# A fused attention and token-MLP kernel: the condition's load and one pair of token tiles on ScalarE's queue, idle matmuls in four pieces in front of the first columns, and a new order of all steps

## The chip, the core and the metric

The kernel runs on one core of one Trainium2 chip. The metric is the device time of one execution in microseconds (us). The core has five engines with an instruction stream each: TensorE (PE in the profile, its weight loads PEld), VectorE (DVE), ScalarE (ACT), GpSimd (POOL) and SyncE (SP). Each runs its own stream in order and waits on semaphores for the others. DMAs are issued here from SyncE's queue (SPq) and, for a few loads and stores, from ScalarE's (ACTq).

## What is computed

One adaLN block over a sequence of S = 2048 tokens of D = 512 channels in bfloat16: a sliding, dilated local attention (part A), and behind it an MLP that mixes tokens (part B).

```
mod = silu(c) @ w_mod                      # c: 1 x 512; six vectors of 512
sa, ca, ga, sb, cb, gb = mod
h = layernorm(x) * (1 + ca) + sa
q, k, v = h @ wqkv                         # 32 heads of 16
logits[s, w] = q[s] . k[s - 2w] / 4        # w = 0..7, masked where s - 2w < 0
x = x + ga * (softmax(logits) over the 8 keys, times v) @ wo
h = layernorm(x) * (1 + cb) + sb
u = gelu(layernorm(h)^T @ w1 + b1)         # over tokens: 2048 -> 1792
x = x + gb * (u @ w2 + b2)^T               # 1792 -> 2048
```

## The kernel before

The 2048 tokens are 16 tiles of 128. Part A goes through them in five chunks of 2, 4, 4, 4 and 2 tiles (`SIZES`); part B needs all tokens for each output and is split in three groups of columns of hidden units, accumulated in PSUM, with partial sums parked in SBUF.

At the start the condition `c` is loaded (`ld_c`, into the tile `c_t`), turned into a column by a small matmul (`cps`), and put through silu by an exponential on ScalarE (`silu_exp`) and three steps on VectorE (`silu_dve`). Two sets of 16 one-column matmuls (`modcols1`, `modcols0`; the tile `psS<-sc,big`) make the scale `a1col` and the shift `sab`; the third part of the modulation is made later as rows (`modrow0`, `modrow1`). `act_table` is an explicit load of ScalarE's function table (ACT_TABLE_LOAD).

For each chunk: statistics of each tile (`ln1s`, `ln1v`: BATCH_NORM_STATS2 and BATCH_NORM_AGGREGATE on VectorE, or two accumulating activations into `junk` on ScalarE), `rstd`, `nb`, normalized tiles (`n1`, into `h`), transposes by TensorE (`tr`, `psS<-ident,h`), evictions of them (`hT`), twelve projections or fewer (`qkv`), their evictions (`ev`, into `q_sb`, `k_f`, `v_sb`; `qvb` is the bias that stems from the shift). Then, on VectorE, four products of query and shifted keys of all eight windows (`qk`, the tile `big<-q_sb,k_f`: 128 x 4096 elements in chunks of four tiles, 128 x 2048 in chunks of two), summed over a head's channels by TensorE (`red`, `psL<-big,group`), the softmax (`max`, `sub`, `exp`, `esum`, `rcp`, `smB`), copies of the weights (`a2`, DMA) and of the values (`vd`, DMA) in the layout of the second product, four products with values (`pv`, `big<-a2sb,vD`) and their sums by TensorE (`pvacc`), the output projection (`wo`, `psS<-woq,o_sb`) with the residual added through the identity, and the layer norms of part B (`x1`, `ln2`, `n2`, `aff`, `ln3`, `h3`). Part B is `mlp1` (with `park`, `inj`, `padd`, `gelu`), then `mlp2`, `fin` and `st_out`.

All steps are written down as entries of a graph by `add` and `add_any`; an entry of `add_any` has alternatives on several engines. `dma2` adds a load that may be issued from SyncE's or ScalarE's queue. The order is not planned at run time: `schedule` (line 86) walks the string `ORDER` (lines 191 to 248) and issues the steps in that order; each engine's stream is the order of its own tokens. A letter behind a token picks the engine (`a`, `d`, `p`, `s` for ScalarE, VectorE, GpSimd, SyncE); for a step of TensorE, `q` does it as four matmuls of 32 columns each, which run at the same time in the four column groups, and `n` leaves out a matmul for the residual, which VectorE then adds. PSUM slots (six), the four `big` and five `vD` slots are given out in the order of the tokens.

The token `fill:N` puts idle matmuls on TensorE, N pieces of 128 columns of the identity by itself, in matmuls of four pieces and a remainder of single ones (`fill_fn`, line 528):

```
for r in [4] * (n // 4) + [1] * (n % 4):
    nc.tensor.matmul(psS[k][:, 0:r * P], lhsT=ident[:], rhs=ident[:]..., start=True, stop=True)
```

All instructions are recorded at line 142, where a helper passes them on, so in the profile the tiles' names tell the steps apart.

Of the kernel before, what the change touches and what calls it, by code (L numbers as in the profile page):

```python
# [13 lines left out]
P = 128  # L14
S, D, H, DH, NW, DIL, F = 2048, 512, 32, 16, 8, 2, 1792
# [27 lines left out]
class _Graph:  # L43
# [7 lines left out]
    def add(self, eng, dur, fn, **kw):  # L51
        return self.add_any([(eng, dur, fn)], **kw)
# [149 lines left out]
ev1_02:a biascols n1_6:p ld_wrow1 rcp0 smB0 ev1_12:a ld_x_4_14 ln1s14:a qkv1_22 qk1_2 a2_0_2:a xt6 ld_wrow3 modrow1
red1_1 a2_0_1:a n1_9:p wsc2_0:d ln1s15:a ln1v14 nb1_3 n1_11:a qkv1_23:q mrows1 qkv1_21 ev1_21:a red1_2 red1_3 xt8
ev1_23:a fill:1 n1_10:p qkv1_20 ev1_20:a ev1_22:a qkv2_13 qkv2_10 wsc0_1:p vd0_2 ev2_13:a ln1v15 vd0_1 max1 sub1
qkv2_00 exp1 a2_0_0:s a2_0_3:s pv0_1 vd0_0 pv0_0 st_row0 pv0_2 qkv2_03 esum1:q ld_wo3 pvacc0_0 vd0_3 halo_v2:p
biascols_cp:a pvacc0_1 pv0_3 pvacc0_2 pvacc0_3 ev2_10:a ev2_00:a qk2_0 n1_13:a n1_12:a ld_row0 woq_s rcp1 smB1
oev0_2:a qkv2_11 qkv2_02:q ev2_03:a qk2_3 qkv2_01:q red2_0 oev0_0:a wo0:q wsc2_1:a wsc2_2:a qkv2_12 ev2_11:a ev2_01:a
ev2_02:a ev2_12:a wo1 qkv2_21:q a2_1_1:a qkv2_22 x1_1:a ln2q1:a x1_0:a xt10 ln2q0:a qk2_1 qkv2_23 xt12 qk2_2 a2_1_0:s
halo_k3:a ln2m0 vd1_2 a2_1_2:s qkv3_12 a2_1_3:s pv1_2 rstd1_4 red2_1 nb1_4 vd1_0 st_row1 red2_2 red2_3 rstd2_0
ev2_22:a nb2_0 ev2_21:a qkv3_13:q ev3_13:a max2 vd1_3 pv1_0 n1_14:a vd1_1 pvacc1_2 n1_15:a qkv2_20:q ev2_20:a sub2  # L210
qkv3_22:q ev3_12:a pv1_1 qkv3_10 exp2 ev2_23:a halo_v3:a qkv3_20 n2_0:a oev1_2:a ev3_10:a esum2 rcp2 qkv3_00 ev3_22:a
qkv3_02:q ev3_00:a pv1_3 ev3_02:a pvacc1_0 ev3_20:a qkv3_01:q ev3_01:a qkv3_11:q xt14 ld_row1 n2_1:p vd2_3 pvacc1_1
smB2 aff0 qk3_0 vd2_1 fill:1 vd2_0 oev1_0:a oev1_1:a pvacc1_3 ev3_11:a qk3_1 qkv3_23:q oev1_3:a a2_2_2:s ln3s1:a
qkv3_03:q wo4 a2_2_1:s qk3_2 a2_2_0:s ev3_03:a ev3_23:a x1_4:a ln2q4:a wo2 x1_2:a a2_2_3:s red3_0 wo3:q x1_3:a ln2q3:a
qkv3_21:q ev3_21:a wo5 red3_1 pv2_3 x1_5:a vd2_2 qk3_3 qkv4_20:q red3_2 qkv4_22 red3_3 qkv4_12 fill:18 ln2q5:a
ld_w1_0_512 ln2q2:a ln2m2 pv2_0 pvacc2_0 vd3_0 ev4_20:a ln3s0:a ln3v0 ev4_12:a rstd2_2 ev4_22:a ln3v1 qkv4_02 oev2_0:a
ln2m4 rstd2_4 nb2_2 n2_2:a max3 sub3:q exp3 pvacc2_3 oev2_3:a qkv4_10:q pv2_2 vd3_2 esum3 nb2_4 pv2_1 vd3_1 n2_3:p
ld_w1_0_0 n2_5:a rcp3 smB3 pvacc2_2 fill:14 a2_3_0:s a2_3_1:s a2_3_3:s n2_4:a qkv4_00:q oev2_2:a rstd3_0 aff2 pvacc2_1
oev2_1:a wo6 wo9 wo7 aff4 nb3_0 ln3s2:d ev4_02:a ln3s3:a ln3v3 h3_1:p wo8 a2_3_2:s ev4_00:a ln3v2 ld_w2_0 ln3s4:d
rstd3_2 nb3_2 x1_9:a ln3s5:a h3_0:p mlp1_0_6_0:q x1_7:a ln3v4 x1_8:a h3_3:d mlp1_0_1_0 h3_2:d mlp1_0_6_2 mlp1_0_1_2  # L220
pv3_1 mlp1_0_5_0:q ln3v5 ev4_10:a ld_w1_0_896 x1_6:a mlp1_0_3_0:q mlp1_0_3_2:q ln2q7:a pvacc3_1 rstd3_4 mlp1_0_5_2:q
oev3_1:a mlp1_0_2_0:q pv3_0 mlp1_0_2_2:q nb3_4 h3_4:a mlp1_0_0_0:q mlp1_0_0_2 h3_5:a mlp1_0_0_4:q qk4_0 ln2q8:a
ln2q6:a park0_0:a ln2q9:a mlp1_0_6_4:q mlp1_0_2_4:q mlp1_0_1_4:q park0_1:a pv3_2 mlp1_0_5_4:q vd3_3 pvacc3_0 oev3_0:a
mlp1_0_3_4:q ld_w2_1 park0_2:a pv3_3 red4_0 ln2m6 pvacc3_2 oev3_2:a mlp1_0_4_0:q qk4_1 pvacc3_3 ld_w1_0_1152
mlp1_0_4_2:q mlp1_0_4_4:q rstd2_6 oev3_3:a wo12:q halo_v4:p vd4_2 vd4_3 nb2_6 n2_9:a qk4_2 n2_7:d qk4_3 wo10:qn red4_1
ld_w1_0_1408 n2_6:a vd4_1 n2_8:a aff6 red4_2 red4_3 max4 park0_3:a ln3s8:d ln3s6:d x1_12:a ln3v8 wo11 vd4_0 ln3s9:d
mlp1_0_7_0 ld_w2_3 park0_4:a ln3v6 mlp1_0_7_2 park0_5:a ln3v9 x1_11:a ln2q12:a mlp1_0_8_0 mlp1_0_8_2 park0_6:a wo13:n
ln3s7:a ln3v7 sub4 mlp1_0_10_0 mlp1_0_9_0 x1_13:d exp4 rstd3_6 nb3_6 esum4 mlp1_0_8_4 ln2q13:a ln2m12 mlp1_0_10_2
mlp1_0_10_4 mlp1_0_9_2 rcp4 mlp1_0_7_4 h3_8:d rstd2_12 mlp1_0_12_0 mlp1_0_12_2 mlp1_0_12_4 smB4 a2_4_1:a a2_4_0:s
mlp1_0_9_4 a2_4_2:s h3_9:d a2_4_3:a h3_7:d nb2_12 h3_6:p mlp1_0_7_6 ln2q11:a park0_7:a x1_10:d mlp1_0_8_6 ld_w1_0_1664  # L230
ln2q10:a park0_8:a n2_13:p mlp1_0_9_6 park0_9:a n2_12:d aff12 ln2m10 rstd2_10 mlp1_0_10_6 park0_10:a ln3s13:a pv4_2
nb2_10 ld_w1_1_0 pv4_1 mlp1_0_11_0 mlp1_0_11_2 mlp1_0_11_4 mlp1_0_12_6 pv4_0 mlp1_0_11_6 ld_w1_1_640 inj1_6:qn pv4_3
pvacc4_0 pvacc4_1 n2_11:a mlp1_0_13_0:q pvacc4_2 pvacc4_3 n2_10:a mlp1_0_13_2:q park0_11:a mlp1_0_13_4 oev4_0:a
# [12 lines left out]
st_out6_0 fin7_0 mlp2_10_0 fin10_0 st_out7_0 mlp2_11_0 mlp2_5_0 st_out1_0 fin5_0 st_out5_0 mlp2_14_0 fin11_0
st_out10_0 st_out11_0 ld_w2_15 fpre mlp2_9_0 mlp2_13_0 fin14_0 st_out14_0 st_out8_0 mlp2_12_0 fin9_0 st_out9_0 fin13_0
st_out13_0 mlp2_15_0 fin12_0 st_out12_0 fin15_0 st_out15_0 mlp2_15_1 fin15_1 st_out15_1 mlp2_15_2 fin15_2 st_out15_2
"""


@with_exitstack
def kernel(
    ctx: ExitStack,
    tc: tile.TileContext,
    A_x: bass.AP,
    A_wqkv: bass.AP,
    A_wo: bass.AP,
# [26 lines left out]
    nc = _OrderedNC(tc, 1)  # L285
# [44 lines left out]
    mask = T([32, NW, PAD], BF, "mask")  # L330
# [745 lines left out]
```

## Time and profile before

| | us |
|---|---|
| median of 3 timed runs | 201.56 (201.33 to 201.79) |
| the profiled execution | 202.11 |
| its span, first to last instruction | 200.4 |
| busy: PE / DVE / ACT / POOL | 191.0 / 159.6 / 128.6 / 18.6 |
| mean granted TensorE clock | 1.000 |

Busy time and share of the span are those of one profiled execution. The times of the timeline are counted from the first instruction, so 1.7 us of the execution's time lie around the span. PE counts idle matmuls as busy. "[0.37 <-ACT q_sb]" means that the engine stood idle for 0.37 us ahead of the instruction and that the last thing to come was ScalarE's write of `q_sb`; "<-issue" is idle time that the profile ascribes to no wait. Matmuls overlap, so their rate is read from the distance of their starts, not from their durations. Some records of matmuls are missing, so counts behind "x" can be low.

### The profile page before, as it was taken

What the parts mean: (1) busy time and instruction counts of PE and PEld (TensorE: products, weight loads), DVE (VectorE), ACT (ScalarE), POOL (GpSimd) and SP (SyncE); (2) the same over time, 40 slices, a digit from 0 to 9 for tenths busy, and PEclk for the clock granted to TensorE, in tenths of its full rate; (3) what the DMA queues carried; (4) which work ended last, traced back from release to release, by engine and by line L of the source; (5) the groups of instructions that cost most, each with busy time, mean ns of one, the idle gap of its engine ahead of it and who ended that gap; (6) DMA issues with size and microseconds to landing.
All of it is one profiled execution on the core that took longest, in us unless ns stands there. A gap on an engine that the chain in (4) does not pass through costs nothing.

```text
span 200.4 us, 4572 instructions
## 1 busy us (share of the span) xinstructions
PE 191.0 (95%) x1818; PEld 95.8 (48%) x1836; DVE 159.6 (80%) x241; ACT 128.6 (64%) x306; POOL 18.6 (9%) x45
## 2 busy tenths in 40 slices
PE   3999999999899999999999999999999999999993
PEld 1387754554344455534444444444444444444453
DVE  2689999999999999999999999986655253726554
ACT  4879897998899999999999698953670000000000
POOL 4155001200100001030000200320000000000000
PEclk9999999999999999999999999999999999999999
DMA  5999594826758745549399268568999201011611
GB/s 161 341 355 350 176 240 127 160 56 185 300 143 321 220 167 194 176 112 311 64 310 257 36 184 196 160 186 234 338 244 298 85 26 52 27 52 52 174 52 52
DMA packets 53889, 35.95 MB, mean 179 GB/s; under 512 B 24428, under 2 KB 50668, under 8 KB 53868
## 3 DMA queue, kind: packets, MB, share of 16 engines
q1 hardware_dynamic: 52228, 35.21, 61.2%
q10 hardware_dynamic: 1640, 0.46, 1.0%
q8 instruction: 14, 0.23, 0.5%
q14 instruction: 7, 0.06, 0.1%
HBM read 22.55 MB, written 2.10 MB: 123 GB/s over the span
## 4 chain that ended last, share of the span: by engine, by line
PE 69%; DVE 22%; issue 4%; DMA 1%; ACT 1%; ACTq 0%; DVEq 0%
PE psS L142 67%; DVE big L142 14%; PE psL L142 3%; DVE st L142 2%; DVE h L142 2%; DMA c_t<-in_c_dram 1%; DVE mv L142 1%; ACT h L142 1%; DVE lsb L142 1%; DVE m L142 1%; DVE nb L142 0%; ACTq L142 0%; DVE woq L142 0%; DVE hT L142 0%; ACT rb L142 0%
## 5 line engine op out<-in xcount | busy, mean ns | idle before, releaser
L142 PEld LDWEIGHTS <-wst 128*128 128x128 bf16 (+1 forms) x536 | 34.9, 101 | 33.7 <-issue 4.0
L142 PE MATMUL psS<-h,wst 128*128 128x512 bf16 (+1 forms) x333 | 50.3, 380 | 0.5 <-issue 0.3
L142 DVE TENSOR_TENSOR big<-q_sb,k_f 128x4096 bf16<-128x4096 bf16 (+1 forms) x20 | 36.6, 1859 | 0.4 <-ACT q_sb L142 0.4
L142 DVE TENSOR_TENSOR big<-a2sb,vD 128x4096 bf16<-128x4096 bf16 (+1 forms) x20 | 36.5, 1860 | 0.2
L142 PE MATMUL psS<-hT,w_qkv 128*32 128x512 bf16 (+3 forms) x360 | 29.7, 346 | 0.0
L142 DVE SCALAR_TENSOR_TENSOR h<-psS,bcol,rows_bc 128x512 f32<-128x512 f32 (+2 forms) x17 | 12.1, 710 | 22.1 <-PE psS L142 20.6
L142 PEld LDWEIGHTS <-w_qkv 128*32 128x32 bf16 (+1 forms) x402 | 19.4, 109 | 17.8 <-issue 4.4
L142 PE MATMUL psS<-gT,big 128*128 128x512 bf16 x110 | 24.7, 379 | 0.1
L142 PEld LDWEIGHTS <-big 128*128 128x128 bf16 x144 | 12.0, 97 | 13.5
L142 ACT ACTIVATE junk<-xx 128x512 bf16<-128x512 bf16 x26 | 16.3, 627 | 3.3 <-DVE xx L142 1.4
L142 PE MATMUL psS<-woq,o_sb 128*32 128x512 bf16 (+1 forms) x107 | 15.7, 380 | 0.9 <-ACT o_sb L142 0.6
L142 ACT ACTIVATE gT<-psS,bcol 128x512 bf16<-128x512 f32 x14 | 9.0, 685 | 8.1 <-DVE psS L142 8.0
L142 POOL TENSOR_SCALAR h<-xx,rs,nb 128x512 bf16<-128x512 bf16 x9 | 6.9, 766 | 75.6 <-DVE nb L142 36.5
L142 DVE TENSOR_TENSOR psS<-psS,gT 128x512 f32<-128x512 f32 x14 | 9.3, 695 | 5.0 <-PE psS L142 5.0
L142 ACT ACTIVATE h<-xx,nb,rs 128x512 bf16<-128x512 bf16 x16 | 12.4, 808 | 0.5 <-DVE nb L142 0.4
L142 PEld LDWEIGHTS <-ident 128*32 128x32 bf16 (+1 forms) x137 | 7.0, 102 | 10.5 <-issue 5.9
L142 PE MATMUL psS<-ident 128*128 128x512 bf16 (+1 forms) x35 | 10.6, 450 | 1.4 <-POOL epscol L142 1.4
L142 PE MATMUL psS<-hT,wst 128*32 128x512 bf16 (+2 forms) x110 | 11.7, 352 | 0.1
L142 DVE TENSOR_TENSOR h<-h,xx 128x512 bf16<-128x512 f32 (+2 forms) x17 | 11.1, 653 | 0.6
L142 DVE TENSOR_TENSOR h<-h,rows_bc 128x1024 bf16<-128x1024 bf16 (+2 forms) x16 | 10.9, 689 | 0.4
L142 DVE BATCH_NORM_STATS2 st<-xx 128x6 f32<-128x512 bf16 x12 | 7.9, 680 | 3.9 <-DMA xx<-in_A_x_dram 3.8
L142 ACT ACTIVATE v_sb<-psS,qvb 128x512 bf16<-128x512 f32 (+1 forms) x20 | 11.0, 595 | 0.0
(100 smaller groups left out, 242.9 us busy)
## 6 DMA issues: line engine op xcount, KB each, us to landing
vD<-v_sb SPq DMA_DIRECT2D x12, 524.5 KB, 4.0
big<-in_B_w_dram SPq DMA_DIRECT2D x4, 896.0 KB, 7.4
vD<-v_sb SPq DMA_DIRECT2D x8, 268.5 KB, 3.8
wst<-in_B_w_dram SPq DMA_DIRECT2D x3, 640.0 KB, 5.0
out_dram<-h SPq DMA_DIRECT2D x15, 128.0 KB, 1.8
wst<-in_B_w_dram SPq DMA_DIRECT2D x2, 800.0 KB, 4.8
xx<-in_A_x_dram SPq DMA_DIRECT2D x6, 256.0 KB, 7.9
gT<-in_w_mod_dram SPq DMA_DIRECT2D x4, 384.0 KB, 5.9
```

The lines of the kernel that those rows point to most:

```text
L142: r = fn(*a, **k)
```

## The change

The condition's load becomes a `dma2` entry like the loads of the first two tiles. The new order starts ScalarE's stream with the table load, the condition's load and the load of tiles 2 and 3 (`ld_x_1_2`), in this order; before, it was tiles 2 and 3, the condition, the table load. All other loads are issued from SyncE's queue as before, in a new order. In front of the condition's matmul stand 14 idle pieces for 4, between it and the first columns 30 and 46 for 64 and 4, in the middle of the kernel 4, 15 and 5 for 1, 1, 18 and 14 (the fill of 13 in the head becomes one of 14). The whole order string is replaced; steps change places within what the graph allows, and some change their engine (`n1_2` and `n1_3` leave VectorE, `ln1s8` and `qvb_cp0` go to it). The diff, cut to the head, the places round VectorE's last products, and `ld_c`:

```
 ORDER = """
-ident ld_x_1_2:a halo0 ld_c consts ld_x1:s ld_x0:s ld_x_1_4:s act_table ln1s3:d fill:4 cps ld_wmod1 silu_exp silu_dve
-fill:64 ln1s1:a ln1s2:a ln1s0:d ln1v1 ld_x_2_8 ln1v0 ln1s4:d ld_wqkv0 rstd1_0 nb1_0 n1_1:a fill:4 ln1v4 n1_0:p ln1s5:d
-ln1v2 ln1v5 ln1v3 rstd1_1 nb1_1 ld_x_2_6 modcols1 n1_2:d n1_5:d ln1s8:a a1col wsc0_3:p n1_4:d tr0_0 hT0_1:a hT0_3:a
-n1_3:d hT0_0:a fill:13 hT0_2:a ld_wqkv1 ld_wmod0 ln1s9:d ld_x_3_10 ln1s6:d tr1_0 tr1_2 hT1_2:a ln1v6 qkv0_02 ln1v9
-hT1_0:a qkv0_12 qkv0_10 ln1s7:d ln1v7 ln1v8 rstd1_2 hT1_3:d wsc1_0:a ev0_12:a modcols0 sab:a ld_x_3_12 nb1_2 n1_8:a
-qkv0_00 qvb0 wsc0_0:p ev0_10:a ld_b2 ld_wo1 hT1_1:d qkv1_00 ln1s11:d ln1s10:d ln1s13:d qkv1_10:q ln1v11 ln1v10
-qvb_cp0:a ev0_00:a ln1s12:a ev0_02:d qkv1_13 ld_wqkv2 qkv0_20 ln1v13 qk0_3 qk0_2 ev1_13:a qk0_0 qvb1 ln1v12 qkv0_22:q
...
-mlp1_0_4_2:q mlp1_0_4_4:q rstd2_6 oev3_3:a wo12:q halo_v4:p vd4_2 vd4_3 nb2_6 n2_9:a qk4_2 n2_7:d qk4_3 wo10:qn red4_1
-ld_w1_0_1408 n2_6:a vd4_1 n2_8:a aff6 red4_2 red4_3 max4 park0_3:a ln3s8:d ln3s6:d x1_12:a ln3v8 wo11 vd4_0 ln3s9:d
...
+act_table ld_c:a ident ld_x1:s fill:14 cps ld_x0:s ld_x_1_4:s ld_wmod1 ld_x_1_2:a ld_x_2_6 silu_exp ld_wqkv0 silu_dve
+ln1s0:d ln1v0 fill:30 ln1s1:a ln1v1 consts rstd1_0 ln1s3:d ld_x_2_8 ln1v3 ld_wqkv1 ln1s2:a nb1_0 fill:46 n1_0:p
+ln1s5:d ln1s4:d ld_wmod0 ld_x_3_10 n1_1:a tr0_0 ln1v5 ln1v4 ln1v2 rstd1_1 modcols1 nb1_1 n1_2:p n1_3:a n1_4:d ln1s6:d
+a1col hT0_0:a hT0_2:a n1_5:d fill:14 hT0_1:a ld_x_3_12 tr1_2 ln1s7:d ln1v6 ld_wqkv2 halo0 ln1s8:d ln1s9:d wsc0_1:p
+ln1v8 hT0_3:a tr1_0 hT1_0:a wsc0_2:p qkv0_02 ln1v7 ln1v9 ld_x_4_14 ld_wrow0 ld_b2 hT1_2:d wsc0_3:a rstd1_2 hT1_1:a
+qkv0_00 ld_wrow1 nb1_2 n1_8:p hT1_3:d ln1s11:d ld_wrow3 ln1s10:d n1_7:p qkv0_12 n1_9:a wsc1_2:a ln1s13:d ln1v11
+qkv0_10 ln1v13 ev0_12:a modcols0 sab:a qvb0 ln1s12:a qvb_cp0:d ev0_00:a ev0_10:a ln1v10 qkv1_10 ev1_10:a ev0_02:d
+wsc0_0:a qkv1_13 ev1_13:a ld_wo3 ld_b1 ln1v12 qkv0_20 rstd1_3 qkv0_22 qk0_3 wsc1_1:a qkv1_00 ev1_00:a qk0_1 qk0_0 qvb1
...
+park0_3:a qk4_0 qk4_3 ld_w2_3 n2_7:d n2_8:a n2_6:a wo11 qk4_2 mlp1_0_5_4:q park0_4:a park0_5:a wo10:qn red4_0 aff6
+x1_11:a wo12:q x1_12:a red4_1 red4_2 red4_3 max4 park0_6:a ld_w1_0_896 vd4_2 mlp1_0_7_0 mlp1_0_7_2 ln3s8:d
...
@@
-    add("act", 0.55, lambda: nc.scalar.dma_start(c_t[:], c[0].rearrange("(t p) -> t p", p=P)), writes=["c_t"],
-        name="ld_c", lat=2.0)
+    dma2(c_t[:], c[0].rearrange("(t p) -> t p", p=P), D * 4, ["c_t"], "ld_c")
```

More of the change, by code (lines that the diff above doesn't have):

```diff
@@ L202 @@
[L202 to L221, printed above, removed]
@@ new lines @@
+n1_15:a ev3_13:a ld_row1 qkv3_02:q ev3_02:a max2 pvacc1_2 ev2_20:a sub2:q pv1_3 qkv3_21:q oev1_2:a qkv3_10 exp2
+qkv2_23 vd1_0 ev3_21:a biascols ev2_21:a pv1_0 esum2 ev2_23:a biascols_cp:a ev3_10:a xt14 vd2_1 rcp2 qkv3_12 n2_0:a
+vd2_3 qkv3_01:q ev3_01:a halo_k3:a qkv3_00 ev3_00:a pv1_1 pvacc1_1 ev3_12:a pvacc1_3 pvacc1_0 smB2 a2_2_1:s ld_w1_0_0
+a2_2_2:s vd2_2 n2_1:p qkv3_03:q oev1_3:a oev1_1:a oev1_0:a qkv4_12 aff0 ln3s1:a ev3_03:a qk3_0 wo5 x1_5:a qk3_2 wo2
+x1_2:a ln2q5:a qkv3_20 ev3_20:a wo4:q halo_v3:p wo3:q red3_0 qkv4_22 qk3_1 red3_1 ln3s0:a red3_2 fill:4 ln3v1 qk3_3
@@ new lines @@
+a2_2_0:s a2_2_3:s pv2_3 ln3v0 x1_3:a ln2q3:a ln2q2:a ln2m2 x1_4:a ln2q4:a ev4_12:a vd2_0 pv2_0 qkv4_00:q ev4_22:a
+rstd2_2 qkv3_23:q ev3_23:a ev4_00:a red3_3 ld_w1_0_512 qkv3_22:q ev3_22:a vd3_1 qkv4_20:q vd3_3 pvacc2_3 nb2_2 n2_2:a
+oev2_3:a max3 qkv4_02:q ln2m4 rstd3_0 n2_3:p sub3:q halo_v4:p pvacc2_0 rstd2_4 vd3_0 exp3 esum3 ev4_20:a pv2_2
+pvacc2_2 nb2_4 rcp3 pv2_1 oev2_2:a vd3_2 fill:15 oev2_0:a smB3 a2_3_3:s qkv4_10 aff2 n2_4:a n2_5:a fill:5 aff4 nb3_0
+h3_1:p h3_0:p a2_3_2:s pvacc2_1 oev2_1:a wo9 ev4_02:a wo7 ln3s2:d ln3s3:a x1_9:a ln3v3 ln3v2 rstd3_2 wo8 x1_7:a wo6
@@ new lines @@
+padd1_10 mlp1_1_9_10 ld_w1_1_1408 gelu10 park1_5:+ mlp1_1_7_10 park1_6:+ mlp1_2_1_11 padd1_9 mlp1_2_1_14 padd2_1 gelu8
+mlp1_2_2_11 padd1_7 gelu7 mlp1_2_2_14 padd2_2 mlp1_2_0_11 mlp1_2_0_14 padd2_0 gelu1 mlp1_2_4_11 mlp1_2_4_14
+mlp1_2_3_11 mlp1_2_3_14 ld_w1_2_640 mlp1_1_11_10 padd1_11 gelu9 mlp1_2_5_11 mlp1_2_5_14 gelu2 mlp1_2_6_11 gelu11
+mlp1_1_12_10 gelu0 padd2_5 gelu5 mlp1_1_13_10 ld_w2_0 padd2_3 gelu3 padd2_4 gelu4 padd2_6 gelu6 mlp2_0_0 mlp2_0_0b
+ld_w2_4 padd1_13 ld_w2_7 ld_w2_9 gelu13 ld_w2_11 padd1_12 gelu12 mlp2_0_0c gsc mlp2_2_0 fin2_0 mlp2_4_0 st_out2_0
@@ L249 @@
+mlp2_6_0 fin6_0 ld_w2_13 st_out6_0 fin0_0 st_out0_0 mlp2_3_0 fin3_0 mlp2_8_0 fin4_0 st_out4_0 fin8_0 st_out8_0
+mlp2_1_0 fin1_0 st_out1_0 mlp2_5_0 mlp2_7_0 st_out3_0 fin7_0 st_out7_0 mlp2_12_0 fin12_0 st_out12_0 ld_w2_15 mlp2_10_0
+fin5_0 st_out5_0 fin10_0 mlp2_9_0 st_out10_0 mlp2_13_0 mlp2_11_0 fin9_0 st_out9_0 fin13_0 st_out13_0 fin11_0
+st_out11_0 mlp2_14_0 fin14_0 st_out14_0 mlp2_15_0 fin15_0 mlp2_15_1 st_out15_0 fin15_1 st_out15_1 mlp2_15_2 fin15_2
+st_out15_2
 """
```

56 lines of the change are left out of this document (28 added, 28 removed).

## The prediction, made before the changed kernel ran

> **What bounds the kernel now.** I read the page first, then the windows, then the timeline at both ends of each stretch. The page gives busy time by engine and the chain of waits by engine:
>
> ```profile
> PE 191.0 (95%) x1818; PEld 95.8 (48%) x1836; DVE 159.6 (80%) x241; ACT 128.6 (64%) x306; POOL 18.6 (9%) x45
> PEclk9999999999999999999999999999999999999999
> PE 69%; DVE 22%; issue 4%; DMA 1%; ACT 1%; ACTq 0%; DVEq 0%
> ```
>
> TensorE looks like the bound of the whole, and the granted clock is full in every slice. Both are averages. The windows (columns: stretch, length, then busy time of PE, PEld, DVE, ACT, POOL) split it:
>
> ```profile
> 0.00:20.00 20.00, 16.49 (x148) 10.08 (x150) 13.09 (x39) 15.20 (x38) 8.80 (x31) 1.00 0.94 301
> 20.00:50.00 30.00, 29.67 (x465) 16.00 (x468) 29.60 (x28) 27.00 (x62) 2.00 (x3) 1.00 0.66 157
> 50.00:80.00 30.00, 29.17 (x377) 14.58 (x381) 29.58 (x28) 28.39 (x69) 1.53 (x2) 1.00 0.66 224
> 80.00:104.00 24.00, 23.08 (x346) 11.38 (x338) 23.81 (x31) 23.22 (x59) 1.70 (x3) 1.00 0.70 192
> 104.00:120.00 16.00, 15.76 (x84) 7.17 (x89) 15.55 (x34) 13.83 (x39) 1.53 (x2) 1.00 0.63 165
> 120.00:160.00 40.00, 39.68 (x219) 18.32 (x216) 27.42 (x55) 20.94 (x44) 3.03 (x4) 1.00 0.81 220
> 160.00:197.00 37.00, 36.84 (x196) 18.18 (x198) 20.00 (x30) 0.00 (x0) 0.00 (x0) 1.00 0.21 62
> ```
>
> From 20 to 104 us VectorE is busy for 82.99 of 84.00 us and TensorE for 81.92; a TensorE that fills its time with idle matmuls counts as busy, so there VectorE, which has none, is the bound. From 120 on VectorE has room (27.42 of 40, then 20.00 of 37) and TensorE has not (39.68 and 36.84). So three stretches count: a head up to VectorE's first large product, VectorE's stretch, and TensorE's. Their borders are in the timeline (start, duration, engine, operation, count, idle before and what ended it):
>
> ```profile
> 0.82 0.48 ACTq L142 DMA_DIRECT2D xx<-in_A_x_dram  x1
> 1.33 0.61 ACTq L142 DMA_DIRECT2D c_t<-in_c_dram  x1
> 1.43 0.61 PE L142 MATMUL psS<-ident 128*128 128x512 bf16 x1 [1.43 <-POOL epscol L142]
> 1.98 1.28 ACT L142 ACT_TABLE_LOAD   x1 [1.98 <-issue]
> 3.98 0.18 PE L142 MATMUL psS<-ident,c_t 4*128 4x4 bf16 x1 [1.94 <-DMA c_t<-in_c_dram]
> 4.10 6.58 PE L142 MATMUL psS<-ident 128*128 128x512 bf16 x17
> 7.90 0.81 ACT L142 ACTIVATE h<-xx,nb,rs 128x512 bf16<-128x512 bf16 x1 [0.23 <-DVE nb L142]
> 7.97 0.77 POOL L142 TENSOR_SCALAR h<-xx,rs,nb 128x512 bf16<-128x512 bf16 x1 [4.73 <-DVE nb L142]
> 9.19 0.15 PEld L142 LDWEIGHTS <-ident 128*128 128x128 bf16 x1 [0.28 <-issue]
> 9.62 0.57 PEld L142 LDWEIGHTS <-ident 128*128 128x128 bf16 x3 [0.28 <-issue]
> 10.52 0.54 PE L142 MATMUL psS<-sc,big 128*128 128x1 bf16 x16
> 10.92 0.61 PE L142 MATMUL psS<-ident,h 128*128 128x128 bf16 x8
> ...
> 18.61 0.17 DVE L142 BATCH_NORM_AGGREGATE mv<-st 128x2 f32<-128x6 f32 x1
> 18.80 1.23 DVE L142 TENSOR_TENSOR big<-q_sb,k_f 128x2048 bf16<-128x2048 bf16 x1
> ...
> 102.87 1.22 DVE L142 TENSOR_TENSOR big<-q_sb,k_f 128x2048 bf16<-128x2048 bf16 x1
> 104.14 0.40 PE L142 MATMUL psL<-big,group 128*32 128x512 bf16 x4 [0.29 <-DVE big L142]
> 105.34 0.38 PE L142 MATMUL psS<-xx,ident 128*128 128x512 bf16 x1
> 105.56 0.81 PE L142 MATMUL psS<-h,wst 128*128 128x512 bf16 x3
> ```
>
> The head: one idle matmul at 1.43, then TensorE waits 1.94 us for the condition, whose load was issued second on ScalarE's queue. After it come 68 idle pieces (of 128 columns; 17 matmuls of four). Their weight loads stand 0.43 us apart up to 9.62 (9.19 to 9.62) and then three come in 0.57 us, so a piece took 0.107 us up to about 9.6 and half of that behind: later a matmul of four pieces takes 0.22 us (105.34 to 105.56), 0.054 a piece. It adds up: 13 matmuls of 0.427 from 4.10 end at 9.65, four of 0.216 at 10.51, and the modulation columns start at 10.52. PEclk doesn't show this; the spacing does. The columns and the first transposes open everything up to 18.80, 8.28 us later, where VectorE's stretch begins. It ends with the last query-key product (102.87 plus 1.22, 104.09), for which TensorE waits 0.29.
>
> **The head, changed.** The condition's load moves ahead of the pair on ScalarE's queue, the table load ahead of both. A fill of 14 pieces (three matmuls of four, two of one) stands before the condition's matmul in place of 4, and 30 and 46 stand behind it in place of 64 and 4: 76 for 68. The fill of 14 runs from 1.43 for 3 x 0.427 + 2 x 0.107 = 1.50, to 2.93. The condition can be issued at 0.82 instead of 1.33, if the table load doesn't hold the queue. That a DMA is issued on this queue while ScalarE still computes, the trace shows once:
>
> ```profile
> 31.12 0.63 ACT L142 ACTIVATE junk<-xx 128x512 bf16<-128x512 bf16 x1
> 31.59 0.74 ACTq L142 DMA_DIRECT2D a2sb<-lsb  x1
> ```
>
> Behind a table load it shows none. I take the row there is, and keep the other end for the rivals. Landing took this chain (start, duration, what), behind the pair's packets on the same queue:
>
> ```profile
> 1.33 2.60 DMA c_t<-in_c_dram
> ```
>
> Ahead of the pair it takes 2.60 at most: it lands by 3.42, and not before the fill is nearly through if it takes 2 us; I take 3.2, the idle pieces start at 3.35. When does a piece become cheap? In before, 5.6 us after TensorE's unbroken work began (3.98 to 9.62). With TensorE busy from 1.43, but for a gap of some tenths, the same 5.6 us end at 7.1: (7.1 - 3.35) / 0.107 = 35 pieces dear, 41 cheap, 2.2 us, and the transposes start at 9.3. They can't start earlier than the first normalized tiles, 8.74 at the latest (7.97 + 0.77), so nothing waits for them. From there to VectorE's first large product the new order has the same TensorE work (columns, 14 pieces for 13, two transposes, four projections, the second columns, the bias product): 8.28 (10.52 to 18.80) + 0.05 for the piece. One more variance step of 0.17 stands between on VectorE, like the one at 18.61. That is 9.3 + 8.5 = 17.8 instead of 18.80: **-1.0 us**.
>
> A rule speaks to this. The Trainium skill ("TensorE: Matmul & The Clock Gate", Part 1) has the array at half clock until one window of about 3.4 us was busy, the window running free of the program. Both piece times above agree with its two clocks; by it a kernel busy from 1.43 turns fast between 4.8 and 8.3, on the mean 6.6, which would put the transposes at 9.05 and the sum 0.25 lower, an estimate from that page.
>
> The pair on ScalarE's queue now lands about half a us later and is read by statistics that in the new order stand behind the first pair's; the fill covers them. Without that cover each 0.7 us of a statistics step on VectorE would go on the head.
>
> **VectorE's stretch.** Counting VectorE's steps from its first to its last query-key product in both orders, the heavy ones (twelve and eight products, at these durations) are the same, and the engine choices that differ cancel (scalings and normalizations swapped one for one). Two normalizations and one statistics step that change engine all lie in the head.
>
> ```profile
> L142 DVE TENSOR_TENSOR big<-q_sb,k_f 128x4096 bf16<-128x4096 bf16 x12 | 27.1, 2286 | 0.4 <-ACT q_sb L142 0.4
> L142 DVE TENSOR_TENSOR big<-a2sb,vD 128x4096 bf16<-128x4096 bf16 x12 | 27.2, 2286 | 0.1
> 28.93 2.29 DVE L142 TENSOR_TENSOR big<-q_sb,k_f 128x4096 bf16<-128x4096 bf16 x1 [0.37 <-ACT q_sb L142]
> ```
>
> The one wait of size, 0.37 at 28.93, is for a projection that stands earlier in the new order. Between 0 and -0.37, I take **-0.2**. What is dropped of TensorE's work here (24 idle pieces in the middle instead of 34, and four fewer switches between matmuls of 32 and of 128 columns, each about 0.1: 104.14 and four such matmuls of 0.054 end at 104.36, the next starts 0.11 later) gains nothing, since VectorE covers it: costed at nothing.
>
> **TensorE's stretch.** From the last reductions to the end, the new order has five matmuls of four pieces fewer: one output projection with its residual (the kind that ends at 105.56 in the rows above) moved ahead of them, into TensorE's spare time: 5 x 0.216 = 1.08. But on the way TensorE meets VectorE once more, at the last attention sums:
>
> ```profile
> 117.03 3.49 DVE L142 TENSOR_TENSOR big<-a2sb,vD 128x2048 bf16<-128x2048 bf16 x3
> 119.68 0.34 PEld L142 LDWEIGHTS <-group 128*32 128x32 bf16 x16 [0.42 <-DVE big L142]
> ```
>
> The second of those three products ends at about 117.03 + 1.13 + 1.22 = 119.38, and TensorE takes it up at 119.68. VectorE's work between 104.09 and there is the same in both orders, so TensorE can come earlier by at most 119.68 - 119.43 = 0.25: **-0.25** of the 1.08; the rest becomes a wait. Behind it the matmuls are the same in number, and so is the store at the end.
>
> **Sum.** -1.0 - 0.2 - 0.25 = -1.45. The profiled execution took 202.11 us (span 200.4 and 1.7 around it): 200.65. The three timed runs have a median of 201.56, 0.55 less, and nothing says in which stretch. If it is spread or lies around the span, the new median is 201.56 - 1.45 = 200.1; if the timed runs lose it in the head, where the moment of the cheaper pieces can move, the gain is smaller and the new median is 200.65. I take the middle, **200.4**, with 199.9 to 201.1 for this case.
>
> **Rivals.** *The condition stuck behind the table load (slower).* ScalarE's queue now begins with it. For it: before has its DMAs issued ahead of the load (0.82, 1.33, then 1.98), so no row shows one passing it. Against it: 31.59 above. Then c is issued at 0.82 + 1.28 = 2.10 and lands 2.2 to 2.6 later, near 4.4; TensorE idles from 2.93, as it did before; cheap pieces come 5.6 us later, at 10.0; of the 76 pieces from 4.5, 51 are dear and 25 cheap (1.35), and the transposes start at 11.35: +0.85 + 0.2 on the head, less 0.45 later, 202.15 to 202.7, as above by the two readings of the runs; 202.4. It decides from a landing of about 4.0 on. The Trainium skill ("ScalarE: Activation LUTs", What ACT_TABLE_LOAD costs) adds a drain of some 1.38 us to a load of 1.28; the 1.28 agrees with the trace, the drain is not to be seen in it (ScalarE's next step at 4.20 waits for TensorE), and if a DMA waited for it too, this rival would be worse by as much.
>
> *The early idle matmuls bring nothing.* The piece becomes cheap at 9.6 as before, whatever came ahead. Then 58 of 76 pieces are dear and 18 cheap, the transposes start at 10.55, the product at 19.05: +0.25, less 0.45, about 201.6 by one reading and 201.9 by the other: no change. For it: one execution shows one such moment only. The same time results if the head gains 1.0 and a projection in VectorE's stretch comes late by that; its wait at 28.93 shows that this place is tight.
>
> *Everything falls out well.* Cheap pieces by 5, the transposes at the tiles' 8.74 (-1.6), the 0.37 gone, the meeting at 119.68 a quarter earlier: -2.2, 199.35 to 199.9, 199.6.
>
> **How the numbers follow.** Chances: forecast 0.47, all well 0.13, no gain 0.14, stuck behind the table load 0.26. A measurement here tells 0.2%, 0.4 us, from no change. Faster is the first two: 0.60; same 0.14; slower 0.26. The range reaches from the all-well case's low end, 199.4, to the slower case, 202.5.
>
> **What would show it.** Right: the condition's matmul near 3.2 with no long wait, weight loads of idle pieces closing up near 7, transposes near 9.3, VectorE's first 2048-wide product near 17.8, its last near 102.9 and then a wait of some 0.8 us at the last attention sums. Wrong: a DMA of c issued at the table load's end, TensorE idle from 2.9 past 4; or a first product near 17.8 with VectorE idle behind it; or a last wait that is absent, so that the whole 1.08 counts.

## The result, and the profile after

| | before | after |
|---|---|---|
| median of 4 timed runs each (us) | 201.44 (201.25 to 201.79) | 202.88 (202.50 to 203.16) |
| ratio, with its 95% interval | | 1.0066 [1.0046, 1.0087] |
| profiled execution (us) | 202.11 | 202.50 |
| its span (us) | 200.39 | 200.40 |

The change made the kernel slower by 0.66%, 1.4 us; 200.4 was forecast. The two profiled executions lie closer to each other (0.39 us) than the medians: the one of before lies above all four of its timed runs, the one of after is the lowest of its four. So the traces are read below by the length of each stretch, over all runs of a kind, and not by one difference of spans.

The page of after, against the same lines of before:

```profile
PE 192.9 (96%) x1818; PEld 96.5 (48%) x1818; DVE 158.6 (79%) x241; ACT 126.8 (63%) x302; POOL 19.1 (10%) x46
PEclk9999999999999999999999999999999999999999
PE 69%; DVE 16%; ACT 7%; DMA 4%; issue 2%; DVEq 0%; SPq 0%
```

Busy times tell little: VectorE has 1.0 us less, and TensorE 1.9 us more, part of which is missing records (before has 1,818 matmuls for 1,836 weight loads; its second trace, below, has all 1,836 and 192.1 us). The chain does: DMA stands for 4% of it instead of 1%, and ScalarE for 7% instead of 1%. The head in the timeline shows both:

```profile
0.81 1.28 ACT L142 ACT_TABLE_LOAD   x1 [0.81 <-PEq L1060]
0.84 0.57 ACTq L142 DMA_DIRECT2D c_t<-in_c_dram  x1
1.45 0.41 ACTq L142 DMA_DIRECT2D xx<-in_A_x_dram  x1
3.04 0.18 PE L142 MATMUL psS<-ident,c_t 4*128 4x4 bf16 x1
6.11 0.36 PEld L142 LDWEIGHTS <-ident 128*128 128x128 bf16 x3 [0.28 <-issue]
6.38 0.69 DVE L142 BATCH_NORM_STATS2 st<-xx 128x6 f32<-128x512 bf16 x1 [1.33 <-DMA xx<-in_A_x_dram]
6.71 2.26 PEld L142 LDWEIGHTS <-ident 128*128 128x128 bf16 x11 [0.23 <-issue]
8.97 0.61 PE L142 MATMUL psS<-ident,h 128*128 128x128 bf16 x8
18.12 4.63 DVE L142 TENSOR_TENSOR big<-q_sb,k_f 128x2048 bf16<-128x2048 bf16 x4
```

The condition is issued at 0.84 while the table load runs from 0.81 to 2.09: the queue does not wait for it. The condition has landed by 2.2, and its matmul runs at 3.04 without a long wait. The idle pieces become cheap at about 6.6: the three weight loads from 6.11 belong to the two single pieces that end the fill of 30, still 0.11 us each, and to the first matmul of four of the next fill; that one takes 0.38 us, and from 6.71 on the loads stand 0.22 apart. The transposes start at 8.97. But the pair that now follows the condition is used only at 6.38, where VectorE had waited 1.33 us for it; in before its first statistics ran at 3.82. The chain of work that ended last now begins with this load (start, duration, what):

```profile
1.45 4.90 DMA xx<-in_A_x_dram
```

The first large product starts at 18.12 instead of 18.80.

At the other border, in the same view:

```profile
102.02 1.21 DVE L142 TENSOR_TENSOR big<-q_sb,k_f 128x2048 bf16<-128x2048 bf16 x1
116.02 1.22 DVE L142 TENSOR_TENSOR big<-a2sb,vD 128x2048 bf16<-128x2048 bf16 x1 [0.80 <-DMA a2sb<-lsb]
119.64 0.84 PE L142 MATMUL psS<-big,group 128*32 128x256 bf16 x24 [0.61 <-DVE big L142]
```

The last query-key product ends at 103.23 instead of 104.09, 0.86 us earlier. The first of the last four products with values then waits 0.80 us for the copies of the attention weights, a wait that before does not have (it started at 115.71 with none), and TensorE starts the last sums at 119.64 instead of 119.68. All of the 0.86 is gone there. In the chain it is this piece (start, duration, what):

```profile
111.96 3.87 DMA a2sb<-lsb
```

Why so long? The four copies of the last chunk are issued from two queues, and the trace records the sixteen increments by which each of them is counted as landed. For the two later copies (times in us):

```
kernel   copy             issued   1st part   15th part   16th part
before   ScalarE's queue  112.70   114.48     114.67      114.70
before   SyncE's queue    112.73   114.75     114.95      114.97
after    ScalarE's queue  111.93   113.71     113.96      115.52
after    SyncE's queue    111.96   114.01     114.23      115.83
```

Fifteen parts land as they did before; one is 1.6 us late. The DMA view, cut to the time of these copies (queue, packets, MB, share), shows what else was there. First before, 112.0 to 115.0, then after, 111.3 to 116.0:

```profile
q1 hardware_dynamic: 570, 0.07, 14.5%
q10 hardware_dynamic: 544, 0.07, 13.7%
```

```profile
q1 hardware_dynamic: 1819, 0.39, 40.6%
q10 hardware_dynamic: 544, 0.07, 9.1%
q8 instruction: 1, 0.02, 1.4%
q14 instruction: 1, 0.01, 0.8%
```

In after there are two instruction fetches: one packet of 16,384 bytes, by the trace's records of packets from 113.21 for 1.03 us, and one of 8,192 bytes, from 113.86 for 0.58 us. In before the nearest 16 KB fetch was at 109.47, ahead of the copies. The window of after is the longer one because its copies end later, and so it takes in more of a weight load (q1).

The fourth thing is outside the span. The profiled executions took 2.10 us more than their span in after and 1.72 in before.

### The profile page after: what moved, and what is told of

Its sections match the earlier page's. It is cut to its first block, busy times and chain, and to the rows that moved or that the text cites. A ratio compares the mean times of both kernels' runs of the same rounds, so it can differ in the third digit from the quotient of the medians.

```text
span 200.4 us, 4557 instructions
## 1 busy us (share of the span) xinstructions
PE 192.9 (96%) x1818; PEld 96.5 (48%) x1818; DVE 158.6 (79%) x241; ACT 126.8 (63%) x302; POOL 19.1 (10%) x46
## 4 chain that ended last, share of the span: by engine, by line
PE 69%; DVE 16%; ACT 7%; DMA 4%; issue 2%; DVEq 0%; SPq 0%
PE psS L142 66%; DVE big L142 8%; PE psL L142 3%; DMA xx<-in_A_x_dram 2%; DVE h L142 2%; DMA a2sb<-lsb 2%; DVE st L142 2%; ACT hT L142 1%; ACT junk L142 1%; DVE m L142 1%; ACT xx L142 1%; DVE lsb L142 1%; DVE mv L142 1%; ACT w_qkv L142 1%; DVE woq L142 1%
## 5 line engine op out<-in xcount | busy, mean ns | idle before, releaser
L142 PE MATMUL psS<-h,wst 128*128 128x512 bf16 (+1 forms) x326 | 50.9, 379 | 0.0
L142 PE MATMUL psS<-woq,o_sb 128*32 128x512 bf16 (+1 forms) x124 | 16.7, 380 | 0.4 <-ACT o_sb L142 0.4
L142 ACT ACTIVATE junk<-xx 128x512 bf16<-128x512 bf16 x24 | 15.1, 628 | 1.7 <-DMA xx<-in_A_x_dram 0.7
L142 POOL TENSOR_SCALAR h<-xx,rs,nb 128x512 bf16<-128x512 bf16 x11 | 8.6, 781 | 68.2 <-DVE nb L142 37.2
L142 ACT ACTIVATE gT<-psS,bcol 128x512 bf16<-128x512 f32 x14 | 8.5, 689 | 9.0 <-DVE psS L142 9.0
L142 PEld LDWEIGHTS <-ident 128*32 128x32 bf16 (+1 forms) x146 | 7.5, 102 | 10.5 <-issue 5.6
L142 ACT ACTIVATE q_sb<-psS,qvb 128x512 bf16<-128x512 f32 (+1 forms) x18 | 10.7, 610 | 1.1 <-PE psS L142 0.8
```

The costliest lines, as they stand in the source:

```text
L142: r = fn(*a, **k)
```

## The experiments

The first theory was that an instruction fetch that meets these copies holds one part of them back, and that the new order moved a fetch into them. Its rivals: the copies wait for the weight load issued at 112.92, or the head is not better at all. Each kernel was timed against before on the same chip.

**Idle matmuls in whole fours.**

```
-fill:14 cps  ...  fill:30  ...  fill:46  ...  fill:14  ...  fill:15  ...  fill:5
+fill:12 cps  ...  fill:32  ...  fill:48  ...  fill:12  ...  fill:16  ...  fill:4
```

> The changed kernel with its idle matmuls counted in whole fours: 12, 32, 48, 12, 4, 16, 4 pieces for 14, 30, 46, 14, 4, 15, 5 - 128 pieces as before it, but 10 matmuls (20 instructions with their weight loads) fewer on TensorE. Theory one (in the profile of the changed kernel the sixteenth part of two of the last copies of the attention weights landed 1.6 us behind the other fifteen, at 115.52 and 115.83, just behind a 16 KB instruction fetch of 1.03 us at 113.21): that fetch comes some 2 us later, the copies land near 114.2, VectorE's wait of 0.80 at 116.02 is gone and TensorE meets it about 0.6 us earlier: 0.5 to 0.7 us less than the changed kernel in the profile. Rival (the copies wait for the weight load issued at 112.92): no change, wait still 0.8.

202.88 us, 1.0059 [1.0038, 1.0079] of before: as the changed kernel. It did not do what it was built for. The 16 KB fetch stood at 113.68, 0.47 later, when the copies also came 0.49 later, and the sixteenth parts landed at 116.21 and 116.46; the wait was 0.94. The first copies had late parts too: the first product with values waited 1.14 us. So it tells nothing apart. The edit takes away 9 matmuls with their 9 weight loads, 18 instructions and not the 20 of the expectation, and that was too few.

**The head alone, put into before.**

```
-ident ld_x_1_2:a halo0 ld_c consts ld_x1:s ld_x0:s ld_x_1_4:s act_table ln1s3:d fill:4 cps
+act_table ld_c ident ld_x_1_2:a halo0 consts ld_x1:s ld_x0:s ld_x_1_4:s ln1s3:d fill:14 cps
```

> The kernel before with the table load and the condition first on ScalarE's queue, tiles 2 and 3 third, and 14 idle pieces for 4 in front of the condition's matmul; the rest of the order as before. If the early condition alone is worth what the changed head won (0.7 us): about 0.3 to 0.7 us faster than before. Rival (the pair on ScalarE's queue lands about 2.5 us later, as at 6.35 in the changed kernel, and here its statistics stand first on VectorE): same or up to 1 us slower.

201.74 us, 0.9986 [0.9959, 1.0014]: no difference that can be told, with single runs from 200.62 to 205.04. Its trace is of an execution of 205.0 us, 3.3 above the median; it shows what that execution looked like, not why the runs differ. In it the columns are done by 8.1, but the first statistics step on VectorE starts at 6.03, where the pair lands, and TensorE has nothing left to do:

```profile
6.03 0.69 DVE L142 BATCH_NORM_STATS2 st<-xx 128x6 f32<-128x512 bf16 x1 [6.03 <-DMA xx<-in_A_x_dram]
7.54 0.55 PE L142 MATMUL psS<-sc,big 128*128 128x1 bf16 x16
9.84 0.62 PE L142 MATMUL psS<-ident,h 128*128 128x128 bf16 x8 [1.75 <-POOL h L142]
12.64 1.78 PE L142 MATMUL psS<-ident,h 128*128 128x128 bf16 x15 [1.13 <-DVE h L142]
```

and on its page the granted clock, in tenths for forty slices:

```profile
PEclk9967999999999999999999999999999999999999
```

In this execution, with waits of 1.75 and 1.13 us, the granted clock drops in the third and fourth slice. That an early condition is worth something only with an order around it that does not need the pair at once, and with fills that reach as far as the data, is argued from this one trace and not shown.

**The old queue and the short first fill, in after.**

```
-act_table ld_c:a ident ld_x1:s fill:14 cps ld_x0:s ld_x_1_4:s ld_wmod1 ld_x_1_2:a ld_x_2_6
+ident ld_x_1_2:a ld_c:a ld_x1:s act_table fill:4 cps ld_x0:s ld_x_1_4:s ld_wmod1 ld_x_2_6
```

> The changed kernel with ScalarE's queue as before (tiles 2 and 3, the condition, the table load) and 4 idle pieces for 14 in front of the condition's matmul; all else of the new order kept. If the new head wins 0.7 us: 0.7 us slower than the changed kernel, about 1% over before. Rival (the late pair costs as much as the early condition wins, as chunk two's statistics wait for it until 6.35): within 0.3 us of the changed kernel, or faster.

203.92 us, 1.0103 [1.0070, 1.0135] of before, 1.04 us over the run in whole fours, which ran on the same chip and is as slow as the changed kernel. So the queue and the first fill are worth about 1 us in the timed runs, which spread from 202.51 to 204.99. The trace (an execution of 203.11 us) shows less: the first product starts at 18.48, 0.36 later than in after and 0.68 later than with whole fours, and the wait at the last products is 1.10 for 0.80 and 0.94. The rest of the order loses more than the head wins.

**More instructions in the head, same columns.** The fill of 46 as single pieces.

```
-for r in [4] * (n // 4) + [1] * (n % 4):
+for r in [1] * n if n == 46 else [4] * (n // 4) + [1] * (n % 4):
```

> The changed kernel with the fill of 46 pieces as 46 matmuls of one piece instead of 11 of four and two of one: the same columns, 66 instructions more on TensorE, so every later instruction fetch of TensorE comes at an earlier point of the program. Theory (a 16 KB fetch that meets the copies of the attention weights holds one of their sixteen parts back): the fetches near 32.5 and 113.2 miss those copies, VectorE's waits of 0.40 at 35.09 and 0.80 at 116.02 go, and the time falls by 0.5 to 1.2 us against the changed kernel (202.9), unless a fetch meets other copies. Rival (the copies wait for other loads): the two waits stay, same time.

201.13 us, 0.9970 [0.9957, 0.9982]: faster than before, where the changed kernel has 1.0066. The 16 KB fetches nearest to the copies went from 32.51 and 113.21 to 31.94 and 106.40. The last copies' sixteenth parts landed at 113.29 and 113.58, with the others, and the last products start with no wait:

```profile
112.83 1.42 DVE L142 TENSOR_TENSOR h<-h,rows_bc 128x1024 bf16<-128x1024 bf16 x2 [0.45 <-ACT h L142]
114.62 1.22 DVE L142 TENSOR_TENSOR big<-a2sb,vD 128x2048 bf16<-128x2048 bf16 x1
118.32 0.84 PE L142 MATMUL psS<-big,group 128*32 128x256 bf16 x24
```

The first copies kept a late part (wait 0.16 instead of 0.40). An 8 KB fetch still lies in the window of the last copies, at 113.22, and holds nothing back. The weight load that the rival blames follows the copies as closely as in after (0.96 us behind the last one's issue in both: 112.29, and 112.92 there), so it was not the cause.

**Three late statistics steps to ScalarE.**

```
-ln3s11:d  ln3s14:d  ln3s15:d
+ln3s11:a  ln3s14:a  ln3s15:a
```

> The changed kernel with three of the last statistics steps (tiles 11, 14, 15 of the third layer norm) on ScalarE instead of VectorE, which has five instructions fewer so (312; the changed kernel has 317, the kernel before 313). Theory: the 8 KB instruction fetch at 202.31, behind the last instruction of the changed kernel and absent in the kernel before, is VectorE's; it goes, and the time around the span falls from 2.1 to 1.7 us: 0.4 us less. Rival (it is another engine's, or it costs nothing): 2.1 stays.

209.69 us, 1.0385 [1.0364, 1.0405]. The 8 KB fetch behind the end is gone, which fits VectorE's stream: the nine other traces of the new order have it, with 316 or 317 records on VectorE, and the five of the old order, with 313, do not. But the time around the span is 2.08, so this fetch was not the cause. The 8 us have another reason. One of the moved steps stands on ScalarE ahead of the evictions of the attention output, and the output projection waits for them:

```profile
122.04 0.63 ACT L142 ACTIVATE junk<-h 128x512 bf16<-128x512 bf16 x1 [3.26 <-DVE h L142]
124.54 1.72 PE L142 MATMUL psS<-woq,o_sb 128*128 128x512 bf16 x4 [3.02 <-ACT o_sb L142]
125.63 0.15 PEld L142 LDWEIGHTS <-wst 128*128 128x128 bf16 x1 [0.28 <-issue]
126.06 0.15 PEld L142 LDWEIGHTS <-wst 128*128 128x128 bf16 x1 [0.28 <-issue]
```

Behind the gap the weight loads stand 0.43 us apart again, the half speed of the head. The Trainium skill ("TensorE: Matmul & The Clock Gate", HAM oscillation) gives gaps over some 3.4 us as what brings this about; here it was a gap of 3.02 us between matmuls, 3.51 between weight loads.

**The fetch moved into the copies, in before.**

```
-mlp1_0_4_0:q mlp1_0_4_2:q mlp1_0_4_4:q
+mlp1_0_4_0 mlp1_0_4_2 mlp1_0_4_4
```

> The kernel before with three MLP steps near 100 us as single matmuls of 128 columns instead of four of 32: 36 instructions fewer on TensorE. Theory of the fetch: the fetch seen at 109.47 comes up to 4 us later and may meet the last copies of the attention weights (112.0 to 115.0): if it does, one part in sixteen lands late, VectorE waits for it near 115.7, and the time rises by up to 1 us; if it doesn't, the time stays within 0.2 us. Rival: no late part whatever the fetch does.

202.51 us, 1.0036 [1.0019, 1.0053]: slower. The 16 KB fetch went from 109.47 to 114.01, for 1.29 us. Fifteen parts of the two later copies landed by 114.78 and 115.05, the sixteenth at 116.51 and 116.78:

```profile
112.08 1.30 ACTq L142 DMA_DIRECT2D a2sb<-lsb  x2
116.97 1.23 DVE L142 TENSOR_TENSOR big<-a2sb,vD 128x2048 bf16<-128x2048 bf16 x1 [1.25 <-DMA a2sb<-lsb]
120.59 0.62 PE L142 MATMUL psS<-big,group 128*32 128x256 bf16 x16 [0.80 <-DVE big L142]
```

A loss of the changed kernel's kind is made in the kernel before, whose order, loads and copies are otherwise untouched. The first product and the last query-key product stand where they stood (18.85, 104.13).

**Before once more.**

> The kernel before once more, for a second trace of it: the timed runs of before go from 201.2 to 202.2, its profiled run took 202.1. If the head's moment of the cheaper idle matmuls makes this spread, the first query-key product lies up to 0.9 us from 18.80 and the rest follows it; if collisions of copies and fetches make it, the first product lies at 18.8 and waits appear later. The time around the span should be 1.7 us again, against 2.1 in the changed kernel.

201.72 us in its one run, span 200.0, 1.72 around it. The first product lies at 18.43 instead of 18.80, and everything behind follows by the same 0.38 (the last sums at 119.30): it is the head that moves from run to run in before.

**Two norms back to their engines,** on top of the single pieces.

```
-n2_12:a n2_13:d
+n2_12:d n2_13:p
```

> The kernel of the run with 66 more instructions, and the second layer norm of tiles 12 and 13 on VectorE and GpSimd, as in the kernel before, instead of ScalarE and VectorE. In the new order VectorE stands idle for 0.45 us near 112.4 for ScalarE's tile, ahead of the last products, which the kernel before did not. If that wait is on the path (TensorE waits for the last products near 118.3): up to 0.3 us faster than that run (201.1), until TensorE's own work is the later. Rival (GpSimd's 0.77 us step is late for the next step instead): no gain.

201.87 us, 1.0016 [0.9989, 1.0043], on another chip than the run with single pieces (0.9970 [0.9957, 0.9982]): not faster, and by these ratios slower. Its timed runs lie between 201.11 and 203.24; the trace is of an execution of 201.12 and doesn't show what makes the others longer. In it the wait of 0.45 is gone, the last products come 0.38 earlier, and the last sums start at 118.33 as in the run with single pieces: TensorE gets there no sooner. There was nothing to win, as VectorE's wait had been covered.

**GpSimd's and SyncE's streams shortened,** on top of that: `halo_v2` and `halo_v3` to ScalarE, and in another kernel five attention copies from SyncE's to ScalarE's queue.

> The kernel of this call's first run with two halo copies of the values on ScalarE instead of GpSimd: GpSimd's stream is four instructions shorter (77, as in the kernel before, where the changed kernel has 79). All kernels with the new order took 2.07 to 2.10 us around their span, all with the old one 1.71 to 1.73. If GpSimd's longer stream is the cause: 1.7 and 0.36 us faster. Rival: 2.1 stays; then SyncE's stream (178 against 173) or something else.

> The kernel of this call's first run with five copies of attention weights of the first two chunks issued from ScalarE's queue instead of SyncE's: SyncE's stream has 176 instructions instead of 178. If SyncE's stream causes the longer time around the span and the limit lies between: 1.7 instead of 2.1. Rival: 2.1 stays. The copies themselves may come later, as ScalarE issues them behind its own work: 0 to 1 us on the span.

202.14 us, 1.0008 [0.9981, 1.0036], and 204.80, 1.0130 [1.0092, 1.0168]. The time around the span stayed at 2.08 and 2.03. In the first, a fetch at 32.60 lies beside the first copies again (a wait of 1.23); in the second, traced in an execution of 207.16 us, the moved copies of the first chunk are issued at 32.1 to 35.2 us, for 30.1 to 31.0 in the kernel it was built on, behind ScalarE's own work.

**The fetch put back, with the single pieces kept.**

```
-mlp1_0_6_4:q mlp1_0_2_4:q ... mlp1_0_3_4:q ... mlp1_0_4_0:q mlp1_0_4_2:q mlp1_0_4_4:q
+mlp1_0_6_4 mlp1_0_2_4 ... mlp1_0_3_4 ... mlp1_0_4_0 mlp1_0_4_2 mlp1_0_4_4
```

> The kernel with the fill of 46 as single pieces (66 instructions more), and six MLP steps between 90 and 102 us as matmuls of 128 columns instead of four of 32: 72 instructions fewer there. The early fetches stay where the first edit put them, the one before the last attention weights goes back to about 113. Theory: the last copies are caught again, VectorE waits 0.8 to 1.2 us near 115, and the time is 0.6 to 1.0 us above the kernel with the single pieces alone (201.1). Rival (what that kernel won came from the single pieces in the head): it stays at 201.1, late part or not.

202.59 us, 1.0050 [1.0035, 1.0065]. The fetch is at 113.46, the sixteenth parts land at 116.10 and 116.31, the wait is 1.04:

```profile
116.50 1.23 DVE L142 TENSOR_TENSOR big<-a2sb,vD 128x2048 bf16<-128x2048 bf16 x1 [1.04 <-DMA a2sb<-lsb]
```

So the single pieces did not win by being single. Of the 1.83 us between the two profiled executions, 1.16 lies between the last query-key product and the last sums, 0.33 in the head and 0.32 in VectorE's stretch.

**The other fill as single pieces,** 42 instructions more.

> The changed kernel with the other fill, of 30 pieces, as single pieces: 42 instructions more on TensorE instead of 66. The fetch near 113.2 comes 42 instructions earlier, some 4 us before the last copies, and misses them: no wait at the last products, 0.6 us less than the changed kernel at least; the early one, near 32, moves by about 1 us and may still meet the first copies. 201.2 to 202.2. Rival (it isn't the place of the fetches): 202.9 as the changed kernel.

201.63 us, 0.9999 [0.9982, 1.0015]. The fetch is at 108.27, the last copies land whole at 113.75 and 114.02, no wait. A fetch at 85.98 now catches a copy of the fourth chunk (late by 1.4 us, a wait of 0.50).

**SyncE's stream made longer, in before:** six small loads more behind the first store.

> The kernel before with six more loads of 3.5 KB each into a spare tile on SyncE's queue, issued behind the first store of the output, near 180 us, where that queue is idle: SyncE's stream has 179 instructions instead of 173 (the changed kernel: 178). If SyncE's longer stream causes the longer time around the span (2.1 us with the new order, 1.7 with the old): 2.1, the span as before, and 0.35 us more. Rival: 1.7 and the time of the kernel before.

201.54 us, 1.0005 [0.9988, 1.0022], and 1.72 around the span: not SyncE's length either.

The lengths of the stretches, from the traces (us; the run with the head alone, the one with GpSimd's stream shortened and those of the late statistics and SyncE's copies left out):

| kernel | first product | first to last query-key product | from there to the last sums | wait at the last products | around the span |
|---|---|---|---|---|---|
| before; again; longer SyncE | 18.80; 18.43; 18.30 | 85.28; 85.27; 85.28 | 15.60; 15.60; 15.60 | none | 1.72 |
| before, fetch moved | 18.85 | 85.28 | 16.46 | 1.25 | 1.73 |
| after | 18.12 | 85.12 | 16.40 | 0.80 | 2.10 |
| after, whole fours | 17.80 | 85.93 | 16.54 | 0.94 | 2.08 |
| after, old queue | 18.48 | 85.08 | 16.71 | 1.10 | 2.08 |
| after, fetch put back | 18.04 | 85.22 | 16.87 | 1.04 | 2.08 |
| after, 46 singles | 17.71 | 84.90 | 15.71 | none | 2.07 |
| after, 46 singles, norms back | 17.94 | 84.68 | 15.71 | none | 2.07 |
| after, 30 singles | 17.63 | 85.49 | 15.58 | none | 2.07 |

All fifteen traces agree on the last copies. In six (after, whole fours, old queue, late statistics, the fetch put back, and before with the fetch moved) a 16 KB fetch begins 0.5 to 1.0 us before the first part of the two later copies lands; the sixteenth part of both is 1.4 to 2.0 us late, and VectorE waits 0.62 to 1.25 us. In the other nine the fetch begins 3.9 us or more ahead, and no part is late by more than 0.1 us. The fetch is TensorE's: in all fifteen it begins when TensorE has 1,358 to 1,373 weight loads behind it.

Not every late part has such a fetch. All five traces of the old order have one in the copies of the third chunk (issued at 62 to 68 us), 0.6 to 2.2 us late, where the fetch began 2.6 to 3.6 us before the first part. VectorE did not wait for these copies, and their cause was not looked for.

## Why the prediction was wrong, step by step

**What held.** The bounds by stretch held: VectorE to the last query-key product, TensorE behind it. The condition lands early (by 2.2, for 3.2) and passes the table load: the slower rival did not occur, and the drain that the Trainium skill ("ScalarE: Activation LUTs", What ACT_TABLE_LOAD costs) adds to a table load held no DMA back here. The cheap pieces begin at about 6.6, not 7.1 as I took and not at 9.6 as the no-change rival had it. By the rule of the Trainium skill ("TensorE: Matmul & The Clock Gate", Part 1) I had estimated 4.8 to 8.3, 6.6 on the mean, and the trace of after agrees (the run in whole fours, at 4.6, lies just outside). The "same 5.6 us" behind the start of TensorE's unbroken work was luck in part: the pieces become cheap at 9.6 in the first trace of before and at 8.8 in the second, and at 5.3 in the run with late statistics, whose head is that of after. The transposes start at 8.97 for 9.3. VectorE's stretch is 0.16 shorter in after and 0.38 in the run with 46 singles, for 0.2; where an earlier chunk's copies come late it is longer than in before, by 0.65 with whole fours and 0.21 with 30 singles.

**The head: near the forecast in size, by a way that was partly wrong.** It was put at -1.0. The first product comes 0.68 earlier in the two first profiles; over the traces it starts at 18.30 to 18.85 with the old head (four) and at 17.29 to 18.12 with the new one (eight traces of the new order; the old queue, 18.48, and the execution of 207.16 us, 19.53, are left out). With the old head it comes 8.28 us behind the columns in all four. The step "8.28 + 0.05 + 0.17" from the transposes to the product was wrong: in after it took 9.15. I had the pair landing "about half a us later" and covered by the fill; its statistics started at 6.38, for 3.82, the second chunk's scale factors came no earlier than in before (9.45 for 9.50), and the chain runs from the pair's load over them and ScalarE. Where the transposes start at 9.03 or later (two traces), 8.6 us follow, about as forecast.

**The failed step: "VectorE's work between 104.09 and there is the same in both orders", -0.25.** VectorE's work is the same, and I took its time to be the same too. The stretch to the last sums became 0.80 longer instead, by a wait that no term and no rival held. The copies of the attention weights were not looked at, because the trace of before shows no wait for them; their slack there was 0.7 us (landed by 114.97, used at 115.71). What used it up was a fetch of TensorE's own instructions, which the new order, with 36 instructions fewer on TensorE, moved by 3.7 us into the copies. It was shown in both directions: taken away in after (46 singles, 30 singles: no wait), made in before (0.36% slower), and put back (0.50% over before).

Nor does the -0.25 appear where the wait is gone: from the last query-key product to the last sums those kernels take 15.58 to 15.71, for 15.60 in before, and TensorE stands in unbroken work in front of the sums. The projection was to move ahead "into TensorE's spare time", and there was none: in after TensorE comes to the last twelve reductions at 104.07, 0.84 us behind the end of the product, where in before it had waited 0.29 for it. Behind the product it has as much to do in both orders, about 71 matmuls of four pieces (four of 32 columns counted as one).

At the first copies the new order waits too, from nothing (norms back, 30 singles) to 1.23 us, and the old one never. A 16 KB fetch lies near them in every trace. In the new order it begins 0.9 to 1.0 us before the first part of the late copies, in the old one about 3 us before (the execution of 207.16 us left out), which is the pattern of the last copies; but no run moved it away, so that this wait comes from it is argued, not shown.

**The failed assumption: the time around the span.** I carried 1.7 us over. It is 2.03 to 2.10 in all ten traces with the new order and 1.72 to 1.73 in all five with the old, 0.36 us, a quarter of the loss. A stream of VectorE shorter than in before, one of GpSimd as short, TensorE's and ScalarE's lengths as they varied, and a longer stream of SyncE in before did not move it. Its cause stays open.

**The range.** Its upper end came from the one slower mechanism I had priced. The profile's +0.39 is the sum of -0.68 in the head, -0.16 in VectorE's stretch, +0.80 to the last sums, +0.05 behind them and +0.38 around the span. The medians differ by 1 us more, as the two profiled executions lie at opposite edges of their timed runs; which stretch that is in was not seen. In the no-gain rival the 201.6 does not follow from its own terms: 201.56 + 0.25 - 0.45 is 201.36.

**The better version.** The changed order with the fill of 46 as single pieces is faster than both: 0.9970 [0.9957, 0.9982] of before, in eight runs on one chip. Against before it wins in the head (first product at 17.71) and in VectorE's stretch (0.38); that its fetch misses the last copies only keeps the loss away, and an edit that changes the number of instructions can bring it back. The gain is small and not secured: two kernels built on it, whose last copies also land whole, came to 1.0016 and 1.0008 on another chip, and the one with 30 singles to 0.9999.

## What to carry to other kernels

Where a trace shows no wait there is still a slack, and a new order should be held against that slack for DMAs as well as for engines: a copy that is used 0.7 us after it lands is a tight one. When an order changes the time by a part of a per cent, look at the instruction fetches beside small, urgent DMAs, and try a few instructions more or fewer before judging the order itself. Compare stretches over several traces, not one span with one span.

## What the runs showed of the hardware that was not expected

- A single 16 KB instruction fetch (1.0 to 1.5 us as one packet) can hold back one of the sixteen parts of a 32 KB copy by 1.4 to 2.0 us, while fifteen land on time; the waiting engine sees what the slack (0.7 us here) does not cover. The Trainium skill ("Runtime: NRT & Kernel Launch", Instruction fetch mechanics) has the crossing of a 16 KB boundary as mostly hidden; here it was hidden from TensorE, which ran matmuls without a wait from 110 to 118 us in after, and not from VectorE.
- 36 to 66 instructions more or fewer on TensorE moved such a fetch by 4.5 to 7 us; 18 fewer moved it by 0.5, as much as the copies moved.
- A DMA behind a table load on ScalarE's queue is issued 0.03 us after the load begins (0.84 against 0.81).
- The same small pair of tiles, issued 0.63 us later (1.45 for 0.82) and behind one other load, was used 2.56 us later (6.38 for 3.82).
- The moment at which idle matmuls become cheap is not fixed: 9.6 and 8.8 us in two executions of the kernel before, 6.6 and 5.3 in two kernels with the same head.
